# A block's opening on one Trainium2 core: tokens transposed before their shift, three heads of the first block first, queues in written order

## The chip, the cores and the metric

The kernel runs on one core of a Trainium2 chip: TensorE (PE) multiplies into PSUM, VectorE (DVE), ScalarE (ACT) and GpSimd (POOL) do the elementwise work, and SyncE (SP) issues the DMAs. One launch computes the whole result from inputs in HBM. The metric is the device time of the launch in microseconds; the time before is 3143.29 us, the median of three runs (3138.22 to 3143.47).

## The reference

A transformer block with adaptive layer norm on x of 2048 tokens by 576 channels, all fp32:

```python
mod = (_silu(c) @ w_mod).reshape(c.shape[0], 6, 1, -1)
sa, ca, ga, sb, cb, gb = ...            # six rows of 576
h = _layernorm(x) * (1 + ca) + sa
x = x + ga * attention(h)               # 32 heads of 128 over 16 K/V groups, the last 512 cached keys
h = _layernorm(x) * (1 + cb) + sb
x = x + gb * ((sigmoid(h @ w_gate) * (h @ w_up)) @ w_down)      # 4608 wide
```

In the attention each head's queries are `h @ wq`, the scores are scaled by `Dh ** -0.5`, a softmax follows over the 512 keys, and the heads' outputs go through `wo`.

## The kernel before, in words

Tokens are in four blocks of 512, each of four tiles of 128; the 576 channels are four chunks of 128 and a tail of 64. Products of fp32 precision are made from three products of rounded halves: an operand is split into a rounded part ("hi", a ScalarE copy) and the rest ("lo", a subtraction on DVE or POOL).

**Opening (lines 79 to 289).** 16 products on zeros warm TensorE up (L90). `silu(c)` is spread over 128 columns (`sbc`, L104), so that a row of w_mod comes out on all partitions: ten fp32 products a row (L282), for scale (m = 1) and then shift (m = 0); DVE copies them out (L285). For block 0, `ln_stats` and `ln_rsqrt` make mean and reciprocal root on DVE, `ln_apply` normalizes, multiplies by scale and adds shift (L176 to L178), and `ln_transpose` turns the tile over on TensorE (L191, L192) and splits it into `hTm` and `hTt` (L194 to L197). The gate row (m = 2) is made otherwise: ScalarE multiplies w_mod by silu(c), POOL sums the chunks, and a product with ones spreads it (`mod_sum`, `mod_half`).

**Attention (lines 292 to 718).** `seq` lists 128 pairs of head and block, the instances b. A step n is one tile i of an instance: b, i = divmod(n, 4). The loop at L702 runs the steps; in step n it calls a quarter of the projection of instance b + 2 (`qproj`; from step -7 on for the first), the scores of tile n + 2, the transposes of the softmax's tile n, a quarter of P times V of the instance before, and two products with Wo of the one before that. `scores` also has DVE's maximum (`neg`, L362) and ScalarE's exponential (`pp`, L364); `transp` has ScalarE's copy and DVE's subtraction (`ptt`, L378, L379). Scores, transposes of P and of K share three PSUM banks (`st`); Wo's products have two (`wo`).

What is done ahead (loads, splits of weights, K and V preparation, the normalization of later blocks) is entered with `at_n(step, function, ...)` in `at_step` and called at the start of its step, before that step's products. Each load takes one of four raw buffers (`raw_tile`, L73), which come free when their last reader is done, in the order of the steps.

```python
at_n(max(q_first(hh) - 16, NLO), load_q, hh)
at_n(max(q_first(hh) - 8, NLO + 1), split_q, hh)
at_n(n - 7, make_k, gg)
norm_block(1, -12, -3, -2, 1, scale, shift, nc.vector, nc.vector)
```

The order on an engine is set by the framework's scheduler, except for instructions given to `tc.keep_in_program_order` (`pin`): these keep the written order among themselves on their engine. Each engine runs its queue strictly in order, and so does SP.

**Background.** While the attention runs, 135 jobs combine and split the weights of the second stage and store them to DRAM (`bg_load` to `bg_store`, L592 to L678), one job every three steps (`slots`, L681), from step 4 in the first half and from step 300 in the second. Every ninth of the first 81 is a "tail" job, which loads four small column blocks in twelve DMAs.

The second stage (from L724) is the gated unit; nothing in it is changed.

## Time and profile before

| what | value |
|---|---|
| median of three runs | 3143.29 us (3138.22 to 3143.47) |
| profiled execution | 3142.64 us, its span 3140.8 us |
| PE busy | 3070.3 us (98%) |
| DVE, ACT, POOL busy | 2165.6, 1455.5, 1561.7 us |
| DMA | 501.73 MB, mean 160 GB/s |

The span is the time from the first instruction to the last of the profiled execution; the 1.8 us around it belong to the launch. TensorE's busy time counts its products with modelled ends, so its share says where it waits, not how near it is to its peak. The first fortieth of the span (78.5 us) is the only one with a busy share of TensorE under eight tenths.

### The profile page before, as it was taken

Reading aid. Unit: us, or ns where it says so; the run is one execution under the profiler, and the core shown is the slowest. Engines: PE = TensorE matmul, PEld = TensorE weight load, DVE = VectorE, ACT = ScalarE, POOL = GpSimd, SP = SyncE. Lnnn points to the kernel's source line nnn. Section 1 sums busy time; section 2 is a strip of 40 time slices with the busy share of each in tenths; the row PEclk is TensorE's granted clock in tenths of the full one; section 3 lists DMA queues with packets and bytes.
Section 4 is the critical chain, followed back from the end, with each engine's and each line's share of the span. In section 5 each row is a group of like instructions: output and inputs, shape, how many; then the busy total and the mean of one; then the engine's idle time right before and its main releaser. Section 6 shows DMA issues by size and latency. Waiting matters only on the chain.

```text
span 3140.8 us, 50879 instructions
## 1 busy us (share of the span) xinstructions
PE 3070.3 (98%) x17012; PEld 2653.1 (84%) x17012; DVE 2165.6 (69%) x4202; ACT 1455.5 (46%) x3189; POOL 1561.7 (50%) x1937
## 2 busy tenths in 40 slices
...
GB/s 143 152 171 149 150 158 173 144 157 154 119 31 94 65 87 154 136 117 125 110 118 111 110 121 253 251 249 214 198 197 202 219 245 200 198 201 198 198 202 119
DMA packets 576740, 501.73 MB, mean 160 GB/s; under 512 B 193504, under 2 KB 456672, under 8 KB 575456
## 3 DMA queue, kind: packets, MB, share of 16 engines
...
q8 instruction: 135, 2.21, 0.3%
...
## 4 chain that ended last, share of the span: by engine, by line
PE 84%; POOL 4%; issue 4%; DVE 3%; DMA 3%; SPq 2%; ACT 1%; POOLq 0%; DVEq 0%; ACTq 0%
PE a L878 14%; PE w L249 12%; PE qp L249 11%; PE wo L249 11%; PE ot L249 10%; PE st L249 9%; PE c L878 7%; PE st L375 6%; PE b L878 3%; SPq L668 1%; DMA raw<-in_A_v_cache_dram 1%; POOL x L657 1%; DVE x L850 0%; POOL hl L809 0%; POOL wb L241 0%
## 5 line engine op out<-in xcount | busy, mean ns | idle before, releaser
L850 DVE TENSOR_TENSOR x<-w,x 128x288 f32<-128x288 f32 x980 | 443.7, 456 | 462.6 <-PE w L249 462.0
L249 PE MATMUL wo<-wb,ov 128*128 128x288 f32 x3072 | 619.7, 310 | 3.7 <-DVE x L402 1.6
L378 ACT ACTIVATE ptt<-st 128x512 fp32r<-128x512 f32 x512 | 305.8, 597 | 619.1 <-PE st L375 618.9
L249 PEld LDWEIGHTS w<-sd,hl 128*128 128x128 f32 x3036 | 514.0, 189 | 89.4 <-POOL hl L809 5.1
L878 PE MATMUL a<-hc,sw 128*128 128x512 f32 x2016 | 583.7, 394 | 2.4 <-DVE v L1015 1.7
L249 PE MATMUL w<-sd,hl 128*128 128x288 f32 x3036 | 563.7, 295 | 3.6 <-POOL hl L809 3.2
L402 DVE SCALAR_TENSOR_TENSOR x<-wo,rs,x 128x288 f32<-128x288 f32 x1024 | 513.3, 512 | 61.6 <-PE wo L249 12.1
L362 DVE TENSOR_REDUCE neg<-st 128x1 f32<-128x512 f32 x512 | 352.6, 689 | 284.2 <-PE st L249 281.7
L249 PEld LDWEIGHTS wo<-wb,ov 128*128 128x128 f32 x3072 | 485.1, 190 | 53.4 <-DVE x L402 3.1
L249 PE MATMUL qp<-hTm,wa 128*128 128x512 f32 x1536 | 446.1, 399 | 6.5 <-DVE qt L346 4.0
L249 PE MATMUL ot<-ptt,vs 128*128 128x512 f32 x1536 | 445.5, 398 | 0.1
L249 PE MATMUL st<-kt,qt 128*128 128x512 f32 x1536 | 438.7, 394 | 0.9 <-DVE hTm L195 0.6
L878 PEld LDWEIGHTS a<-hc,sw 128*128 128x128 f32 x2016 | 355.7, 188 | 42.1 <-DVE v L1015 3.3
L379 DVE TENSOR_TENSOR ptt<-st,ptt 128x512 fp32r<-128x512 f32 x512 | 348.4, 681 | 36.2 <-ACT ptt L378 36.1
L364 ACT ACTIVATE pp<-st,neg 128x512 f32<-128x512 f32 x512 | 349.9, 683 | 33.2 <-DVE neg L362 29.6
L249 PEld LDWEIGHTS st<-kt,qt 128*128 128x128 f32 x1536 | 288.5, 188 | 64.1 <-DVE ptt L379 1.0
L375 PEld LDWEIGHTS st<-ident,pp 128*128 128x128 f32 x2048 | 254.9, 140 | 90.2 <-ACT pp L364 23.3
L375 PE MATMUL st<-ident,pp 128*128 128x128 f32 x2048 | 308.9, 273 | 17.3 <-ACT pp L364 17.0
L878 PE MATMUL c<-hc,sw 128*128 128x512 f32 x1008 | 305.9, 396 | 11.5 <-ACT v L885 11.5
L241 POOL TENSOR_TENSOR wb<-raw,wb 128x576 fp32r<-128x576 f32 x64 | 91.3, 1427 | 448.6 <-ACT wb L237 445.6
L249 PEld LDWEIGHTS qp<-hTm,wa 128*128 128x128 f32 x1536 | 262.8, 190 | 34.1 <-DVE qt L346 5.4
L249 PEld LDWEIGHTS ot<-ptt,vs 128*128 128x128 f32 x1536 | 261.4, 189 | 23.7 <-DVE ptt L379 0.3
...
## 6 DMA issues: line engine op xcount, KB each, us to landing
...
sd<-dsc SPq DMA_DIRECT2D x249, 288.0 KB, 2.9
...
dsc<-x SPq DMA_DIRECT2D x126, 96.0 KB, 2.4
```

The costliest lines, as they stand in the source:

```text
L241: pin(nc.gpsimd.tensor_sub(sp[:, 1, :], raw, f32(sp[:, 0, :])))
L249: nc.tensor.matmul(p, l, r, start=first and n == 0, stop=last and n == len(pairs) - 1)
L362: nc.vector.tensor_reduce(NEG[b][:, i : i + 1], p, axis=AX.X, op=OP.max, negate=True)
L364: nc.scalar.activation(PP[n], p, AF.Exp, bias=NEG[b][:, i : i + 1], accum_out=SUM[b][:, i : i + 1])
L375: nc.tensor.transpose(p[:, k * P : (k + 1) * P], PP[n][:, k * P : (k + 1) * P], ident)
L378: nc.scalar.activation(PT[b][:, 0, :, cols], pv_, AF.Copy)
L379: nc.vector.tensor_sub(PT[b][:, 1, :, cols], pv_, f32(PT[b][:, 0, :, cols]))
L402: nc.vector.scalar_tensor_tensor(xv, p, RS[b][:, i : i + 1], xv, op0=OP.mult, op1=OP.add)
L657: pin(nc.gpsimd.tensor_sub(v.bitcast(F32R), v, hi[:, a:b, :]))
L668: pin(nc.sync.dma_start(wsc[f + q][to * TQ : (to + 1) * TQ, a:b, 4, :], src[rows]))
L850: nc.vector.tensor_add(acc, p, acc)
L878: nc.tensor.matmul(p, l, r, start=first and n == 0, stop=n == len(pairs) - 1, skip_group_check=not first)
```

## The change

- `Ordered` wraps the handle of the engines: while `held[0]` is true, every instruction issued through it is kept in written order. It turns false at step 8; from there only what was pinned before is kept.
- Block 0's tokens are normalized on ScalarE (`ln_scaled`: x times y plus a bias of -mean times y), multiplied by scale, and transposed without the shift. The channels then lie on partitions, and the shift, turned over into columns (`scol`), is added as a per-partition bias when the transposes are copied from PSUM (`ln_shifted`), for a whole chunk of 512 tokens at once. Block 1 goes the same way in steps -1 to 6.
- All w_mod rows, gate too, are made by ten fp32 products; the gate's are spread over the opening and steps -3, 2 and 3. The loads are issued in another order, x in four pieces behind two chunks of w_mod.
- `seq` begins with heads 0, 1 and 2 on block 0, then head 2 on block 1, heads 0 and 1 on block 1, head 3 on both. K's second group is so needed from instance 2 on, prepared at step 4, and heads 0 and 1 need their Wo twice (`inst`: 66 Wo instances where there were 64).
- Steps run from -8 instead of -24, head 3's projection is in steps 7 and 8, the background's first slot is step 7, and 10 warm-up products are left of 16.

```diff
+class Ordered:
...
+    def __init__(self, tc, held, of, deep=True):
+        self._tc, self._held, self._of, self._deep = tc, held, of, deep
+    def __getattr__(self, name):
+        got = getattr(self._of, name)
+        if self._deep:
+            return Ordered(self._tc, self._held, got, False)
+        def call(*args, **kw):
+            i = got(*args, **kw)
+            if self._held[0]:
+                self._tc.keep_in_program_order(i)
+            return i
+        return call
...
-    nc = tc.nc
+    held = [True]
+    nc = Ordered(tc, held, tc.nc)
...
+    def pin(i):
+        if not held[0]:
+            tc.keep_in_program_order(i)
...
-    for k in range(16):
+    for k in range(10):
         nc.tensor.matmul(idle[:, :P], busy, busy, start=True, stop=True)
...
-    load_x(0)
+    sbc = at.tile([P, NC + 1, P], F32, tag="ov", name="sbc", bufs=2)
+    nc.vector.tensor_copy(sbc, cexp[:, :, None].to_broadcast([P, NC + 1, P]))
+    extra = at.tile([P, 4 * P], F32, tag="extra", name="extra")
     scale, shift, gate = mod_rows("scale", wp), mod_rows("shift", wp), mod_rows("gate", wp)
-    wm = {}
-    for m in (1, 0):
-        w = at.tile([P, NC + 1, D], F32, tag="ptt", name="wm0", bufs=2)
-        for k in range(NC + 1):
+    WM, EARLY, HN, NMR = {}, {}, {}, {}
+    def load_mod(m, ks):
+        if m not in WM:
+            WM[m] = at.tile([P, NC + 1, D], F32, tag="ptt", name="wm0", bufs=2)
+        for k in ks:
             kk = P if k < NC else TAIL
-            nc.sync.dma_start(w[:kk, k, :], w_mod[k * P : k * P + kk, m * D : (m + 1) * D])
-        wm[m] = w
+            nc.sync.dma_start(WM[m][:kk, k, :], w_mod[k * P : k * P + kk, m * D : (m + 1) * D])
+    def mod_mm(m, ks, p2):
+        for k in ks:
+            kk = P if k < NC else TAIL
+            for j in range(2):
+                nc.tensor.matmul(p2[j], sbc[:kk, k, :], WM[m][:kk, k, j * D2 : (j + 1) * D2],
+                                 start=(k == 0), stop=(k == NC))
+    def ln_ready(b):
+        ln_rsqrt(b)
+        mv, y = LN[b]
+        NMR[b] = const.tile([P, TPB], F32, tag="ln_a", name="nmr", bufs=2)
+        nc.vector.scalar_tensor_tensor(NMR[b], mv[:, :, 0], -1.0, y, op0=OP.mult, op1=OP.mult)
+    def ln_scaled(b, t, eng):
+        h = wp.tile([P, D], F32, tag="h", name="h", bufs=4)
+        nc.scalar.activation(h, xs[b][:, t, :], AF.Identity, scale=LN[b][1][:, t : t + 1],
+                             bias=NMR[b][:, t : t + 1])
+        eng.tensor_mul(h, h, scale)
+        HN[b, t] = h
+    def ln_tail(b, t):
+        e = extra[:, t * P : (t + 1) * P].rearrange("p (s d) -> p s d", s=2)
+        nc.gpsimd.tensor_copy(e, HN[b, t][:, None, NC * P :].to_broadcast([P, 2, TAIL]))
+    def ln_channels(b, t, k, p):
+        src = HN[b, t][:, k * P : (k + 1) * P] if k < NC else extra[:, t * P : (t + 1) * P]
+        nc.tensor.transpose(p[:, t * P : (t + 1) * P], src, ident)
+    def ln_shifted(b, k, p):
+        main, tail = hTs[b]
+        hi, lo = (main[:, k, :], main[:, NC + k, :]) if k < NC else (tail[:, 0, :], tail[:, 1, :])
+        nc.scalar.activation(hi, p, AF.Identity, bias=scol[:, k : k + 1])
+        nc.vector.scalar_tensor_tensor(lo, p, scol[:, k : k + 1], f32(hi), op0=OP.add, op1=OP.subtract)
...
+    load_mod(1, range(2))
+    for t in range(TPB):
+        nc.sync.dma_start(xs[0][:, t, :], xf[0][:, t, :])
+    load_mod(1, range(2, NC + 1))
+    load_mod(0, range(NC + 1))
+    EARLY["q", 0] = load_a(wq, 0)
+    p2 = [ps_wo(), ps_wo()]
+    mod_mm(1, range(NC + 1), p2)
+    load_mod(2, range(2))
+    EARLY["q", 1] = load_a(wq, DH)
+    EARLY["k"] = load_k0()
+    load_x(1)
+    EARLY["q", 2] = load_a(wq, 2 * DH)
+    load_mod(2, range(2, NC + 1))
     for t in range(TPB):
         ln_stats(0, t)
-    ln_rsqrt(0)
-    for m, row, add in ((1, scale, 1.0), (0, shift, 0.0)):
-        p2 = [ps_wo(), ps_wo()]
+    for j in range(2):
+        nc.scalar.activation(scale[:, j * D2 : (j + 1) * D2], p2[j], AF.Copy, bias=1.0)
+    ln_ready(0)
+    for t in range(TPB):
+        ln_scaled(0, t, nc.vector)
+        ln_tail(0, t)
+    cols = [ps_pt(), ps_pt(), ps_pt(), ps_ot(), ps_ot()]
+    p2 = [ps_wo(), ps_wo()]
+    mod_mm(0, range(NC), p2)
+    for t in range(TPB):
         for k in range(NC + 1):
-            kk = P if k < NC else TAIL
+            ln_channels(0, t, k, cols[k])
+        if t == 0:
+            mod_mm(0, (NC,), p2)
+    nc.scalar.activation(shift[:, :D2], p2[0], AF.Copy)
+    nc.vector.tensor_copy(shift[:, D2:], p2[1])
+    ends = wp.tile([P, 2, TAIL], F32, tag="hd", name="hd", bufs=1)
+    nc.scalar.activation(ends, p2[1][:, None, D2 - TAIL :].to_broadcast([P, 2, TAIL]), AF.Copy)
+    pc = ps_qp()
+    for k in range(NC + 1):
+        src = shift[0:1, k * P : (k + 1) * P] if k < NC else ends.rearrange("p s d -> p (s d)")[0:1, :]
+        nc.tensor.transpose(pc[:, k : k + 1], src, ident[0:1, 0:1])
+    scol = csb
+    nc.vector.tensor_copy(scol, pc[:, : NC + 1])
+    EARLY["sq"] = split_a_hi(EARLY["q", 0])
+    split_a_lo(EARLY["q", 0], EARLY["sq"])
+    new_hT(0)
+    for k in range(NC + 1):
+        ln_shifted(0, k, cols[k])
+    gate2 = [ps_wo(), ps_wo()]
+    mod_mm(2, range(1), gate2)
+    def gate_mm(ks):
+        mod_mm(2, ks, gate2)
+        if NC in ks:
             for j in range(2):
-                nc.tensor.matmul(p2[j], sbc[:kk, k, :], wm[m][:kk, k, j * D2 : (j + 1) * D2],
-                                 start=(k == 0), stop=(k == NC))
-        for j in range(2):
-            nc.vector.tensor_scalar(row[:, j * D2 : (j + 1) * D2], p2[j], add, None, op0=OP.add)
-    new_hT(0)
-    for t in range(TPB):
-        ln_apply(0, t, scale, shift, nc.vector, nc.vector)
-        ln_transpose(0, t)
+                nc.scalar.activation(gate[:, j * D2 : (j + 1) * D2], gate2[j], AF.Copy)
+    def chunks1(ks):
+        if 0 in ks:
+            new_hT(1)
+        for k in ks:
+            p = ps_wide()
+            for t in range(TPB):
+                ln_channels(1, t, k, p)
+            ln_shifted(1, k, p)
...
-            if hd in (0, H - 2):
+            if half == 0 and hd < 4:
+                if hd == 0:
+                    seq += [(0, 0, 0), (0, 1, 0), (0, 2, 0), (0, 2, 1), (0, 0, 1), (0, 1, 1), (0, 3, 0), (0, 3, 1)]
+            elif hd in (0, H - 2):
                 seq += [(half, hd, b0), (half, hd + 1, b0), (half, hd, b1), (half, hd + 1, b1)]
             else:
                 seq += [(half, hd, b0), (half, hd, b1), (half, hd + 1, b0), (half, hd + 1, b1)]
...
-    NLO = -24
+    NLO = -8
...
+    SA[0], RA[1], RA[2], KR[0] = EARLY["sq"], EARLY["q", 1], EARLY["q", 2], EARLY["k"]
+    at_n(-8, load_v, 0)
+    at_n(-4, split_q, 1)
+    at_n(-4, split_q_lo, 1)
+    at_n(-3, make_k, 0)
+    at_n(-3, gate_mm, (1,))
+    at_n(-1, split_q, 2)
+    at_n(-1, split_q_lo, 2)
+    at_n(3, split_q, 3)
+    at_n(3, split_q_lo, 3)
+    for t in range(TPB):
+        at_n(-1 + t // 2, ln_stats, 1, t)
+    at_n(1, ln_ready, 1)
+    for t in range(TPB):
+        at_n(2 + t // 2, ln_scaled, 1, t, nc.vector if t % 2 else nc.gpsimd)
+    at_n(2, gate_mm, (2,))
+    at_n(3, gate_mm, (3, 4))
+    for t in range(TPB):
+        at_n(4, ln_tail, 1, t)
+    at_n(5, chunks1, (0, 1))
+    at_n(6, chunks1, (2, 3, 4))
...
-    for hh in range(1, NH):
-        at_n(max(q_first(hh) - 16, NLO), load_q, hh)
-        at_n(max(q_first(hh) - 8, NLO + 1), split_q, hh)
-        at_n(max(q_first(hh) - 7, NLO + 1), split_q_lo, hh)
+    def o_first(i):
+        return TPB * (inst[i][1] + 2)
+    def o_free(i):
+        return TPB * (inst[i][2] + 3)
+    for hh in range(3, NH):
+        at_n(max(q_first(hh) - 16, -6), load_q, hh)
+        if hh > 3:
+            at_n(q_first(hh) - 8, split_q, hh)
+            at_n(q_first(hh) - 7, split_q_lo, hh)
     for gg in range(2 * HKV):
         n = TPB * first_g[gg]
         if gg:
             at_n(n - 15, load_k, gg)
-            at_n(n - 7, make_k, gg)
+            at_n(n - 7 if gg > 1 else 4, make_k, gg)
             at_n(n - 10, load_v, gg)
-        at_n(n - 2, make_v, gg)
...
-    at_n(-6, mod_fetch, 2)
-    at_n(-3, lambda: mod_sum(wm[2]))
-    for j in range(2):
-        at_n(j, mod_make, gate, 2, j, 0.0)
-    for hh in range(NH):
-        n = max(o_first(hh) - 7, o_free(hh - 2) if hh > 1 else 0)
+        at_n(n - 2 if gg else 1, make_v, gg)
+    for hh in range(len(inst)):
+        n = max(o_first(hh) - 7, o_free(hh - 2) if hh > 1 else 5)
         assert n < o_first(hh)
         at_n(n - 7, load_o, hh)
-        at_n(max(n - 3, 1), scale_o, hh)
+        at_n(max(n - 3, 4), scale_o, hh)
         at_n(n, split_o, hh)
         at_n(n, split_o_lo, hh)
...
-    norm_block(1, -12, -3, -2, 1, scale, shift, nc.vector, nc.vector)
...
-    slots = [(n, 0) for n in range(4, n1 - 43, STEP)] + [(n, 1) for n in range(n1 + 44, N - 14, STEP)]
+    slots = [(n, 0) for n in range(7, n1 - 43, STEP)] + [(n, 1) for n in range(n1 + 44, N - 14, STEP)]
...
+        if n == 2 * TPB:
+            held[0] = False
         for fn, args in at_step.pop(n, ()):
             fn(*args)
         b, i = divmod(n, TPB)
         bq, part = divmod(n - 1, TPB)
-        if ok(bq + 2):
+        if bq + 2 == 3:
+            if n > 6:
+                qproj(3, 2 * (n - 7))
+                qproj(3, 2 * (n - 7) + 1)
+        elif ok(bq + 2):
             qproj(bq + 2, part)
```

How this moves the instructions is shown at three places. Names carry a number where one tile is told from another; L36 is the wrapper's line.

ScalarE in the changed kernel, steps 1 to 4 (`h`: block 1's normalization, `pp`: exponentials, `ptt`: P's hi copy, `wa`: the split of Wq's head 3, `gate`: the gate row):

```order
L36 ACTIVATE h<-x_102,nmr,ln_y 128x576 [waits DMAHW1_49,Pool_49]
L36 ACTIVATE h<-x_102,nmr,ln_y 128x576 [waits Pool_49]
L36 ACTIVATE pp,sum<-st,neg 128x512 [waits DVE_49,PE_49,Activation_49]
L36 ACTIVATE ptt<-st 128x4x128
L36 ACTIVATE wa<-raw 128x640 [waits DMAHW7_49,DMAHW6_49,DMAHW5_49]
L36 ACTIVATE h<-x_102,nmr,ln_y 128x576 [waits Pool_49] x2
L36 ACTIVATE gate<-wo 128x288 [waits PE_49] x2
L36 ACTIVATE pp,sum<-st,neg 128x512 [waits DVE_49,PE_49,Activation_49]
L36 ACTIVATE ptt<-st 128x4x128
L36 ACTIVATE kt<-st 128x512 [waits PE_49]
L36 ACTIVATE qt<-qp 128x512 [waits PE_49]
```

ScalarE before, around its third Wq split (`wa`), among block 1's copies and the modulation's multiplications (`wmt`):

```order
L378 ACTIVATE ptt<-st 128x4x128 [waits PE_49]
L212 ACTIVATE wa<-raw 128x640 [waits DMAHW7_49,DMAHW0_49,Pool_49]
L126 ACTIVATE wmt<-wmt,cexp 64x288 [waits DMAHW3_49,Activation_49]
L185 ACTIVATE hd<-h 128x128 [waits DVE_49]
L126 ACTIVATE wmt<-wmt,cexp 64x288
L364 ACTIVATE pp,sum<-st,neg 128x512 [waits DVE_49]
L194 ACTIVATE hTm<-st 128x4x128 [waits PE_49]
L196 ACTIVATE hTt<-wo 128x128 [waits PE_49]
L237 ACTIVATE wb<-raw 128x576 [waits Pool_49]
L364 ACTIVATE pp,sum<-st,neg 128x512 [waits DVE_49,PE_49]
L378 ACTIVATE ptt<-st 128x4x128
L378 ACTIVATE ptt<-st 128x4x128 [waits PE_49]
```

The split of a Wq head, which stood among other copies, now stands in written order ahead of two normalizations, the gate's copies and the exponential of tile 5.

SP in the changed kernel, from V's first load: `raw_345` is K's second group, `raw_472` is Wq's head 3, which takes the buffer that `raw_345` leaves (its DMA queue 1, and PE's transposes):

```order
L36 DMA raw_343<-in_A_v_cache_dram 128x512 [waits DMAHW0_49,Activation_49,Pool_49]
L36 DMA raw_345<-in_A_k_cache_dram 128x512 [waits DMAHW1_49,Activation_49,Pool_49]
L36 DMA raw_383<-in_A_v_cache_dram 128x512 [waits DMAHW2_49,PE_49]
L36 DMA raw_385<-in_A_wo_dram 128x576 [waits DMAHW3_49,DMAHW4_49,Activation_49,Pool_49]
L36 DMA raw_387<-in_A_wo_dram 128x576 [waits DMAHW0_49,Pool_49]
L36 DMA raw_472<-in_A_wq_dram 128x4x128 [waits DMAHW5_49,DMAHW1_49,PE_49]
L36 DMA raw_472<-in_A_wq_dram 64x128 [waits DMAHW6_49]
L36 DMA raw_472<-in_A_wq_dram 64x128 [waits DMAHW7_49]
```

SP before, from V's first load: `raw_344` and `raw_384` are Wq's second and third head:

```order
L317 DMA raw_342<-in_A_v_cache_dram 128x512 [waits DMAHW2_49,DVE_49,PE_49]
L202 DMA raw_344<-in_A_wq_dram 128x4x128 [waits DMAHW3_49,DVE_49,PE_49]
L204 DMA raw_344<-in_A_wq_dram 64x128 [waits DMAHW4_49]
L204 DMA raw_344<-in_A_wq_dram 64x128 [waits DMAHW5_49]
L118 DMA wmt_396<-in_w_mod_dram 64x576 [waits DMAHW6_49,PE_49,Activation_49]
L202 DMA raw_384<-in_A_wq_dram 128x4x128 [waits DMAHW7_49,DMAHW2_49,Pool_49]
L204 DMA raw_384<-in_A_wq_dram 64x128 [waits DMAHW0_49]
L204 DMA raw_384<-in_A_wq_dram 64x128 [waits DMAHW1_49]
L232 DMA raw_398<-in_A_wo_dram 128x576 [waits PE_49]
```

The load that waited for POOL's split of V in before is, for head 3, now one that waits for TensorE's transposes of K.

DVE in the changed kernel, from the first scores' maximum (`neg`) on: block 1's statistics (`BN_STATS`, `BN_AGGR`) stand between the maxima:

```order
L36 TENSOR_REDUCE neg<-st 128x1 [waits PE_49]
L36 BN_STATS st<-x_102 128x6 [waits DMAHW1_49]
L36 BN_STATS st<-x_102 128x6
L36 BN_AGGR mv<-st 128x2 [waits DVE_49]
L36 BN_STATS st<-x_102 128x6 x2
L36 BN_AGGR mv<-st 128x2 [waits DVE_49]
L36 TENSOR_REDUCE neg<-st 128x1 [waits PE_49]
L36 BN_STATS st<-x_102 128x6 x2
L36 BN_AGGR mv<-st 128x2 [waits DVE_49]
L36 BN_STATS st<-x_102 128x6 x2
L36 BN_AGGR mv<-st 128x2 [waits DVE_49]
L36 SCALAR_TENSOR_TENSOR qt<-qp,qt 128x512 [waits Activation_49]
```

DVE before, from the last copies of block 0 on: the same statistics ahead of any scores:

```order
L195 TENSOR_TENSOR hTm<-st,hTm 128x4x128 [waits Activation_49]
L197 TENSOR_TENSOR hTt<-wo,hTt 128x128 [waits Activation_49]
L326 TENSOR_TENSOR kt<-st,kt 128x512 [waits Activation_49]
L158 BN_AGGR mv<-st 128x2 [waits DVE_49]
L155 BN_STATS st<-x_110 128x6 x2
L155 BN_STATS st<-x_110 128x6 [waits DVE_49]
L158 BN_AGGR mv<-st 128x2 [waits DVE_49]
L155 BN_STATS st<-x_110 128x6
L158 BN_AGGR mv<-st 128x2 [waits DVE_49]
L164 TENSOR_SCALAR ln_v<-mv 128x4 [waits DVE_49]
```

The statistics of block 1 moved from ahead of the first scores to between the first three, and the reciprocal root behind them.

## Rows read from the trace of the kernel before

**Rows 1.** Busy time by stretch; columns: engine busy (instructions), granted clock, DMA share, GB/s.

```profile
0.00:58.50 58.50, 41.52 (x169) 30.39 (x169) 46.26 (x110) 24.18 (x59) 15.92 (x21) 0.85 0.51 158
58.50:200.00 141.50, 141.50 (x798) 121.58 (x799) 105.00 (x193) 88.37 (x206) 77.41 (x110) 1.00 0.50 134
```

**Rows 2.** TensorE's timeline, opening; columns: start us, us, engine line op, idle before.

```profile
8.55 5.28 PE L282 MATMUL wo<-wm,raw 128*128 128x288 f32 x20 [1.28 <-DMA wm<-in_w_mod_dram]
...
29.41 0.80 PE L249 MATMUL qp<-hTm,wa 128*128 128x512 f32 x1 [1.31 <-ACT wa L212]
30.77 5.06 PE L249 MATMUL qp<-hTm,wa 128*128 128x512 f32 x11 [0.56 <-POOL wa L216]
...
44.89 1.63 PE L249 MATMUL st<-kt,qt 128*128 128x512 f32 x3
```

**Rows 3.** TensorE's timeline, after the opening.

```profile
74.83 0.84 PE L249 MATMUL st<-kt,qt 128*128 128x512 f32 x3
...
77.45 0.60 PE L323 MATMUL st<-ident,raw 128*128 128x128 f32 x4
```

**Rows 4.** Chain of waits: start us, us, what.

```profile
70.43 0.44 PE st L375 x4
70.87 0.70 PE ot L249 x3
```

**Rows 5.** Groups of instructions, 0 to 80 us: count | busy us, mean ns | idle before.

```profile
L362 DVE TENSOR_REDUCE neg<-st 128x1 f32<-128x512 f32 x12 | 8.2, 687 | 4.6 <-PE st L249 4.5
L364 ACT ACTIVATE pp<-st,neg 128x512 f32<-128x512 f32 x11 | 7.5, 683 | 0.7 <-DVE neg L362 0.7
...
L379 DVE TENSOR_TENSOR ptt<-st,ptt 128x512 fp32r<-128x512 f32 x9 | 6.2, 688 | 2.4 <-ACT ptt L378 2.4
...
L378 ACT ACTIVATE ptt<-st 128x512 fp32r<-128x512 f32 x10 | 6.0, 598 | 8.5 <-PE st L375 8.5
...
L212 ACT ACTIVATE wa<-raw 128x640 fp32r<-128x640 f32 x4 | 2.8, 729 | 0.0
```

**Rows 6.** DVE's timeline: statistics, reciprocal root, multiplications of blocks 0 and 1.

```profile
7.55 1.18 DVE L155 BATCH_NORM_STATS2 st<-x 128x6 f32<-128x288 f32 x3 [2.17 <-DMA x<-in_A_x_dram]
...
13.20 0.16 DVE L171 SCALAR_TENSOR_TENSOR ln_y<-ln_a,ln_y 128x4 f32<-128x4 f32 x1
...
15.12 1.41 DVE L177 TENSOR_TENSOR h<-h,scale 128x576 f32<-128x576 f32 x2
...
39.89 2.63 DVE L177 TENSOR_TENSOR h<-h,scale 128x576 f32<-128x576 f32 x2
```

**Rows 7.** POOL's timeline beside the last of these.

```profile
37.87 2.77 POOL L129 TENSOR_TENSOR wm<-wm 128x288 f32<-128x288 f32 x3 [4.70 <-ACT wm L126]
```

**Rows 8.** Two-microsecond stretches of the opening; columns as in rows 1.

```profile
20.00:22.00 2.00, 0.85 (x8) 0.81 (x9) 1.97 (x4) 0.50 (x2) 0.00 (x0) 1.00 0.77 252
22.00:24.00 2.00, 1.76 (x10) 0.87 (x8) 1.90 (x5) 2.00 (x7) 0.00 (x0) 0.76 0.43 102
...
28.00:30.00 2.00, 0.69 (x2) 0.29 (x1) 1.82 (x6) 1.86 (x4) 0.56 (x1) 0.50 0.71 180
...
42.00:44.00 2.00, 0.06 (x1) 0.09 (x2) 2.00 (x3) 0.12 (x1) 1.92 (x2) 0.88 0.00 0
44.00:46.00 2.00, 2.00 (x8) 1.81 (x9) 2.00 (x2) 1.62 (x5) 1.84 (x3) 0.50 0.00 0
...
50.00:52.00 2.00, 0.43 (x4) 0.42 (x4) 2.00 (x5) 2.00 (x6) 0.00 (x0) 1.00 0.00 0
```

**Rows 9.** SP's timeline: the two small pieces of a Wq load.

```profile
33.62 1.15 SPq L204 DMA_DIRECT2D raw<-in_A_wq_dram  x2
```

**Rows 10.** Raw buffers, 0 to 60 us: landing times of their loads.

```profile
DMA to landing us min/median/max: 2.3/4.1/7.3
```

**Rows 11.** A stall in the middle of the attention.

```profile
530.00:540.00 10.00, 6.17 (x28) 5.16 (x27) 3.79 (x7) 4.27 (x11) 7.43 (x11) 0.75 0.52 144
```

**Rows 12.** ScalarE's waits from 450 to 800 us: us, times, longest.

```profile
ACT x L652 <- POOL extra L639: 5.0, 1, 5.0
```

50 lines of the change are left out of this document (25 added, 25 removed).

## The prediction

> **What bounds the kernel now.** I read the busy times by stretch first. In the first 58.5 us TensorE is busy 41.5 us at a mean clock of 0.85; in the next 141.5 us it is busy all of them at 1.00 [rows 1]. So from 58.5 us on the end is set by TensorE's own work, and the change, which rearranges the opening, is worth what it shifts the moment from which TensorE never waits, no more. The reader is to see in TensorE's timeline how late that moment comes: first projection at 29.4 us, first scores at 44.9 [rows 2]; the eleventh scores (tile 10) start at 74.8, in the stretch without a gap [rows 3]. I use "tile 10 starts" as the milestone: by then both kernels have done the same attention work, except that the one before still owes the transposes of its second K group (four, at 77.5), 0.44 us at the pitch of the chain of waits, where three products of a 512-column group take 0.70, 0.23 each [rows 3, 4]. So before stands at 75.3 us, and whatever the changed kernel reaches there later or earlier is the change in the end time, all work after it being the same.
>
> **The opening up to the first scores: about 15 us earlier.** A w_mod row is ten products of 0.53 us [rows 2]. With two of its chunks ahead of x in SP's queue and three behind, the first row ends at about 12.5 us (estimate); ScalarE's two copies free its banks at 13.6. Four chunks of the second row take 4.2 us, to 17.8; the transposes of token tile 0, now from the unshifted h, 0.55; the last chunk 1.06; the other three tiles 1.65: 21.1. Five column transposes and a DVE copy end at 21.9, one ScalarE copy and one DVE subtraction (0.60 and 0.69, like the copies of P [rows 5]) open the first projection at 23.4. Before, it started at 29.4 [rows 2]. Fourteen products go at DVE's pace, to 26.7; K's transposes 0.44, one gate chunk 1.06 and seven products 1.6 bring tile 0's scores to 29.9, against 44.9. The six warm-up products left out fall in time that waits for loads anyway: nothing.
>
> **The steps after it: given back.** What was done early (statistics, normalization and transposes of block 1) now lies between the scores, in written order on every queue. With that order each step is one loop through DVE and ScalarE: DVE's maximum of tile n+2 (0.69), ScalarE's exponential (0.69), ScalarE's copy of the transposed tile n (0.60), DVE's subtraction (0.69): 2.7 us with hand-over [rows 5], and what stands between them is added. At full clock TensorE has 1.8 to 3.9 us of work in such a step, so up to step 7 the loop decides, not TensorE.
> - Step 0: scores 0 end at 30.6. Before scores 2's maximum DVE has two more reductions, the statistics of four token tiles and the split of q: the whole of statistics and reciprocal root took 5.8 us for block 0 (7.55 to 13.36) [rows 6], some 3.4 of it the statistics, which I take at 4.0 among the others: maximum done at 37.2, copy of tile 0 done at 38.5.
> - Step 1: loop 2.7 and the root with its thirteen small operations, 2.5: 43.7.
> - Step 2: two ScalarE normalizations 1.2, a DVE multiplication and 2.0 of the loop. The multiplication is 0.71 where POOL is idle and 1.31 where POOL adds [rows 6, 7]; POOL works on its own two tiles here, so I take 1.31: 48.2.
> - Step 3 holds a new wait. ScalarE's next instruction is the split of Wq's head 3. Its load takes the raw buffer of K's second group, so SP can issue it only behind that group's transposes, which stand in step 4, behind DVE's subtraction of tile 2. ScalarE cannot pass it: behind the split stand two normalizations, two gate copies and exponential 5, and TensorE's scores 6 need the bank that exponential 5 frees. Transposes end at 49.4; three DMAs take 1.5 to issue (the last two 1.15 [rows 9]) and 2.3 to 4.1 to land [rows 10]. I take 2.3, since the last ones are the 32 KB pieces: 53.3 (bounds 53.0 and 55.1). ScalarE so stands still for 5 us and TensorE for some 8. Then split 0.73 [rows 5], normalizations 1.2, multiplication 1.3, loop 2.0: 58.5.
> - Step 4: loop and two more subtractions on DVE, K's and q's, each some 0.6 (0.69 less what the next one overlaps): 3.8, 62.3. Step 5: two for block 1's first chunks, 3.8: 66.1. Step 6: three, 4.5: 70.6. Step 7: the bare loop, 2.7: 73.3.
> - Then TensorE's remaining projection of 1.6 us; tile 10 starts at about 75.2.
>
> Against 75.3 that is 0. The 15 us of lead are spent: about 6.5 on statistics and root inside the loop, 5 on the wait for head 3, the rest on block 1's chunks.
>
> **Other parts.** Gate as ten fp32 products instead of two costs some 4 us more of TensorE, all inside steps where the loop is late: nothing; if that cover went, 4. Two more Wo instances (heads 0 and 1 are used twice) add two loads, two POOL multiplications and two splits beside other work, on engines with slack: nothing, 0 to 1. The background work on the second stage's weights begins one slot (three steps) later and takes one slot more in the second half. Its four-column "tail" jobs move by three steps against K's pattern of sixteen. Before, the fifth of them (step 28 + 4 x 27 = 136) sat one step ahead of a K preparation (9 x 16 - 7 = 137), and will be at 139; TensorE lost 3.8 us in those 10 us, at clock 0.75 [rows 11], while ScalarE waited 5.0 us for POOL's sums [rows 12]. That one goes; another may take its place. I bound it by -4 and +4 and take 0.
>
> **Clock.** Before, the granted clock was 0.50 (the 1.2 GHz level) at 28 to 30 us, after TensorE had worked 0.85 of 2 us at 20 to 22, and again at 44 to 46, after 0.06 of 2 at 42 to 44; yet it stayed 1.00 at 50 to 52 with 0.43 of 2 [rows 8]. In the changed order TensorE is busy nearly all the time from 13.6 to 34, so I expect 2.4 GHz for the first projections, and the low level after the wait of 8 us. From scores 6 to 64 us that costs 1.1, to 72 us 3.5; to 60 nothing, the loop being later. I take 1.
> The Trainium skill (TensorE: Matmul & The Clock Gate, "HAM oscillation — how this bites in real kernels") says that waits between bursts throttle the clock, so that each burst begins slow. The first two stretches agree with it, the third doesn't; by the rule the sum is the +1 to +3.5 above, by the third stretch 0.
>
> **Sum.** 0 + 1 = 1 us on the profiled execution's 3142.6 (span 3140.8 and 1.8 around it), which is 0.65 below the median shown; I say 3143.5.
>
> **Rivals.**
> - Faster: the wait for head 3 is short or hidden. Without its 5 us, and without the low clock behind it, tile 10 starts at 69.7, so 5.6 earlier: 3137; with the tail job's 4 us gone as well, 3133. For it: the lead at the first scores is real in every count. Against: the new instruction order shows load, transposes and split in just this dependence, and exponential 5 behind it.
> - Slower: the clock falls to 1.2 GHz at the first projection and comes back only after it, as in the kernel before (0.76 at 22 to 24 us, 0.50 at 28 to 30 [rows 8]). Place: 24 to 36 us; price: 21 products at 0.46 (5.06 us for 11 [rows 2]) instead of 0.23, four transposes and a gate chunk at double, 6 us, all on the path, since the first scores head the loop: 3149.5; with Wq landing at 4.1 us instead of 2.3, 3151. Each us at the low level costs half a us there, so it decides from some 12 us on. For it: TensorE waits around 22 us for the shift's columns. Against: some 1 us of waiting there, where before it had worked 0.85 of 2 us [rows 8].
> - The loop is longer than counted: POOL beside DVE stretches more than the two multiplications. Each 0.6 us on the loop is 0.6 us of time; five such are 3 us: 3146.
>
> **Numbers.** Given back, within some 4 us of 3143.5: 0.66 (its own range 3139 to 3148, with the longer loop in it). Faster: 0.15, of which 0.13 beyond 6.3 us. Slower: 0.19, of which 0.17 beyond. 0.2% of 3143 us, 6.3 us, is about what a measurement of this kernel tells from no change. So faster 0.13, same 0.70, slower 0.17; range 3135 to 3152, which reaches into both rivals and holds the tail job's bounds.
>
> **What would show it.** Right: first scores near 30 us; ScalarE idle for about 5 us before Wq's third-head split, released by a DMA; TensorE idle for 7 to 8 us near 50 to 58 us; the never-waiting stretch beginning past 66 us; tile 10 near 75. Wrong: no such idle time (then faster), or a clock of 0.50 between 24 and 36 us (then slower). The step most open is the landing of Wq and what the clock does behind it; time lost or won behind 80 us, near 530 us first [rows 11], would be the background's part.

## The result: slower by a quarter of a percent, and the profile after

The changed kernel's median is 3150.15 us (3144.04 to 3152.09, seven runs), the kernel before beside it 3138.22 us (3135.7 to 3146.7, seven runs): ratio 1.0025, 95% interval 1.0015 to 1.0034, some 7.8 us. The profiled execution took 3150.36 us, its span 3148.3 against 3140.8. That is inside the range forecast, but it is a loss, and the forecast was none. By the 6.3 us that the prediction itself drew between no change and slower, it lies on the slower side, to which it had given 0.17.

TensorE's timeline of the changed kernel answers to [rows 2, 3]. All instructions that are held in written order show line 36, the wrapper's.

```profile
11.08 7.70 PE L36 MATMUL wo<-wm,sbc 128*128 128x288 f32 x28 [2.75 <-DMA wm<-in_w_mod_dram]
...
24.54 2.99 PE L36 MATMUL qp<-hTm,wa 128*128 128x512 f32 x12 [0.69 <-DVE hTm L36]
...
31.12 0.84 PE L36 MATMUL st<-kt,qt 128*128 128x512 f32 x3
...
51.30 0.66 PE L36 MATMUL st<-ident,raw 128*128 128x128 f32 x4 [0.56 <-DVE ptt L36]
...
60.22 1.65 PE L36 MATMUL st<-kt,qt 128*128 128x512 f32 x3 [7.33 <-ACT pp L36]
...
70.53 0.63 PE L36 MATMUL wo<-ident,extra 128*128 128x128 f32 x4 [2.44 <-DVE hTm L36]
...
73.80 2.40 PE L36 MATMUL qp<-hTm,wa 128*128 128x512 f32 x7
...
79.51 0.86 PE L36 MATMUL st<-kt,qt 128*128 128x512 f32 x3
```

The first scores come at 31.1 us, 13.8 us ahead of before; tile 10's at 79.5, 4.2 us behind the 75.3 of before (with its owed transposes). The lead is spent, and more. From there on both kernels have scores every 3.4 us; at tile 16, where nothing is owed any more, they stand at 100.0 and 95.8, still 4.2 apart. The other 3.3 of the 7.5 us between the spans come later. Tile 16's scores, in the changed kernel and before:

```profile
100.00 0.85 PE L36 MATMUL st<-kt,qt 128*128 128x512 f32 x3
```

```profile
95.84 0.84 PE L249 MATMUL st<-kt,qt 128*128 128x512 f32 x3
```

ScalarE's timeline shows where it went (`pp` the exponential, `ptt` the copy of the transposed tile, `wa` the split of Wq):

```profile
38.30 0.69 ACT L36 ACTIVATE pp<-st,neg 128x512 f32<-128x512 f32 x1 [1.86 <-DVE neg L36]
38.89 0.19 ACT L36 ACTIVATION_READ_ACCUMULATOR pp<-st,neg 128x1 f32 x1
38.98 0.59 ACT L36 ACTIVATE ptt<-st 128x512 fp32r<-128x512 f32 x1
...
44.42 0.69 ACT L36 ACTIVATE pp<-st,neg 128x512 f32<-128x512 f32 x1 [4.33 <-DVE neg L36]
...
49.93 0.59 ACT L36 ACTIVATE ptt<-st 128x512 fp32r<-128x512 f32 x1
55.45 0.74 ACT L36 ACTIVATE wa<-raw 128x640 fp32r<-128x640 f32 x1 [4.93 <-DMA raw<-in_A_wq_dram]
...
59.39 0.69 ACT L36 ACTIVATE pp<-st,neg 128x512 f32<-128x512 f32 x1 [1.10 <-DVE neg L36]
```

Two things stand in it. The split of head 3 waits 4.93 us for its load, and TensorE 7.33 us behind it. And the copy of tile 0, whose transposes ended at 35.4, starts at 38.98: it stands behind the exponential of tile 2, which waits for DVE's maximum. The groups of 0 to 80 us sum that up, against 0.7 us of such waiting of the exponentials and 2.4 of DVE's subtractions before [rows 5]:

```profile
L36 ACT ACTIVATE pp<-st,neg 128x512 f32<-128x512 f32 x10 | 6.9, 688 | 20.2 <-DVE neg L36 19.7 <-PE wo L36 0.4
...
L36 DVE TENSOR_TENSOR ptt<-st,ptt 128x512 fp32r<-128x512 f32 x8 | 5.5, 692 | 9.1 <-ACT ptt L36 9.1
```

By stretch, as in [rows 1, 8, 11]:

```profile
0.00:58.50 58.50, 43.58 (x189) 32.49 (x189) 30.53 (x83) 22.92 (x43) 13.27 (x21) 0.97 0.52 159
58.50:200.00 141.50, 137.34 (x765) 118.53 (x766) 102.99 (x189) 89.81 (x206) 84.37 (x114) 0.97 0.46 126
...
38.00:40.00 2.00, 2.00 (x6) 1.52 (x6) 0.58 (x2) 1.70 (x4) 0.00 (x0) 0.50 0.08 29
...
58.00:60.00 2.00, 0.00 (x0) 0.00 (x0) 1.27 (x2) 0.90 (x3) 1.92 (x3) 0.52 0.43 121
60.00:62.00 2.00, 1.78 (x5) 1.34 (x6) 1.31 (x3) 1.63 (x5) 2.00 (x5) 0.50 0.58 157
...
72.00:74.00 2.00, 2.00 (x8) 1.71 (x7) 1.27 (x2) 1.02 (x3) 1.52 (x2) 0.50 0.83 253
```

```profile
530.00:540.00 10.00, 7.63 (x43) 6.27 (x41) 4.21 (x8) 2.85 (x8) 8.57 (x11) 1.00 0.59 165
540.00:550.00 10.00, 8.51 (x40) 7.22 (x41) 6.78 (x12) 6.13 (x16) 6.48 (x10) 0.83 0.44 122
```

Up to 58.5 us TensorE does more than before and at a better clock; behind it 4.2 us are idle where before had none. The granted clock stands at its lower level (0.50) at 38 to 40, 60 to 64 and 72 to 74 us, behind waits of 2.30, 7.33 and 2.44 us; behind the wait of 2.75 us before 11.08 it stayed at 1.00. Near 530 us TensorE still loses 3.9 us, as it did before (3.83): that stall has only moved.

### The profile page after: what moved, and what is told of

Its sections match the earlier page's. It is cut to its first block, busy times and chain, and to the rows that moved or that the text cites. A ratio compares the mean times of both kernels' runs of the same rounds, so it can differ in the third digit from the quotient of the medians.

```text
span 3148.3 us, 50886 instructions
## 1 busy us (share of the span) xinstructions
PE 3069.1 (97%) x17021; PEld 2653.4 (84%) x17021; DVE 2149.1 (68%) x4176; ACT 1459.5 (46%) x3181; POOL 1566.2 (50%) x1943
## 4 chain that ended last, share of the span: by engine, by line
PE 84%; DVE 4%; POOL 4%; DMA 3%; SPq 2%; issue 2%; ACT 1%; POOLq 0%; ACTq 0%; DVEq 0%
PE st L36 16%; PE a L36 13%; PE w L36 12%; PE wo L36 12%; PE qp L36 11%; PE ot L36 10%; PE c L36 7%; PE b L36 3%; SPq L36 2%; DVE x L36 1%; POOL x L36 1%; DMA ts<-scr 1%; POOL h L36 1%; POOL extra L36 0%; POOL hl L36 0%
## 5 line engine op out<-in xcount | busy, mean ns | idle before, releaser
L36 DVE TENSOR_TENSOR x<-w,x 128x288 f32<-128x288 f32 x980 | 444.6, 457 | 466.3 <-PE w L36 465.1
L36 PE MATMUL wo<-wb,ov 128*128 128x288 f32 x3072 | 619.6, 310 | 4.4 <-DVE ov L36 2.2
L36 PEld LDWEIGHTS w<-sd,hl 128*128 128x128 f32 x3036 | 513.1, 189 | 89.8 <-POOL hl L36 5.4
L36 PE MATMUL a<-hc,sw 128*128 128x512 f32 x2016 | 582.9, 393 | 3.6 <-DVE v L36 2.1
L36 ACT ACTIVATE ptt<-st 128x512 fp32r<-128x512 f32 x512 | 306.2, 598 | 601.4 <-PE st L36 600.7
L36 PE MATMUL w<-sd,hl 128*128 128x288 f32 x3036 | 565.2, 296 | 3.8 <-POOL hl L36 3.5
L36 DVE SCALAR_TENSOR_TENSOR x<-wo,rs,x 128x288 f32<-128x288 f32 x1024 | 513.4, 512 | 58.4 <-PE wo L36 9.4
L36 DVE TENSOR_REDUCE neg<-st 128x1 f32<-128x512 f32 x512 | 352.7, 689 | 278.2 <-PE st L36 276.1
L36 PEld LDWEIGHTS wo<-wb,ov 128*128 128x128 f32 x3072 | 483.8, 189 | 53.7 <-DVE ov L36 3.2
L36 PE MATMUL qp<-hTm,wa 128*128 128x512 f32 x1536 | 446.2, 399 | 5.8 <-DVE qt L36 5.2
L36 PE MATMUL st<-kt,qt 128*128 128x512 f32 x1536 | 438.1, 393 | 7.6 <-ACT pp L36 7.3
L36 PE MATMUL ot<-ptt,vs 128*128 128x512 f32 x1536 | 445.3, 397 | 0.1
L36 PEld LDWEIGHTS a<-hc,sw 128*128 128x128 f32 x2016 | 355.3, 188 | 43.4 <-DVE v L36 3.7
L36 DVE TENSOR_TENSOR ptt<-st,ptt 128x512 fp32r<-128x512 f32 x512 | 348.9, 681 | 44.9 <-ACT ptt L36 44.8
L36 ACT ACTIVATE pp<-st,neg 128x512 f32<-128x512 f32 x512 | 350.2, 684 | 55.1 <-DVE neg L36 52.9
L36 PEld LDWEIGHTS st<-kt,qt 128*128 128x128 f32 x1536 | 289.5, 189 | 72.6 <-ACT pp L36 7.8
L36 PEld LDWEIGHTS st<-ident,pp 128*128 128x128 f32 x2048 | 254.7, 140 | 91.9 <-ACT pp L36 26.1
L36 PE MATMUL st<-ident,pp 128*128 128x128 f32 x2048 | 308.2, 273 | 21.1 <-ACT pp L36 21.0
L36 POOL TENSOR_TENSOR wb<-raw,wb 128x576 fp32r<-128x576 f32 x66 | 94.1, 1427 | 469.5 <-ACT wb L36 469.4
L36 PE MATMUL c<-hc,sw 128*128 128x512 f32 x1008 | 305.3, 396 | 12.0 <-ACT v L36 12.0
L36 POOL TENSOR_TENSOR x<-x,x 128x128 fp32r<-128x128 f32 (+7 forms) x458 | 270.7, 605 | 60.4 <-ACT x L36 39.6
L36 PEld LDWEIGHTS qp<-hTm,wa 128*128 128x128 f32 x1536 | 263.0, 190 | 32.8 <-DVE qt L36 6.5
```

The lines of the kernel that those rows point to most:

```text
L36: i = got(*args, **kw)
```

## The experiments

Times of single executions scatter by several us here, so the table gives the ratio of the runs to those of the kernel before on the same chip, and three distances from each profile: from the first projection (P) to the scores of tiles 8, 10 and 16, which leave out how late P itself is. The ratios' intervals are some 0.0009 to either side, so a difference between two of them is uncertain by some 0.0013, 4 us (an estimate from the intervals shown).

| kernel | ratio, 95% | P, us | P to tile 8 | P to tile 10 | P to tile 16 |
|---|---|---|---|---|---|
| before | 1 | 29.4 | – | 45.9 with the 0.44 owed | 66.4 |
| changed | 1.0025 (1.0015 to 1.0034) | 24.5 | 46.4 | 55.0 | 75.5 |
| late_split | 1.0007 (0.9998 to 1.0016) | 27.6 | 41.7 | 50.8 | 71.4 |
| k1_early | 1.0012 (1.0003 to 1.0021) | 26.3 | 41.0 | 47.9 | 69.0 |
| stats_early | 1.0020 (1.0011 to 1.0029) | 24.3 | 46.2 | 53.2 | 74.2 |
| unheld | 0.9969 (0.9958 to 0.9981) | 27.5 | 28.6 | 36.7 | 59.1 |
| copy_first | 1.0013 (1.0004 to 1.0023) | 23.8 | 42.0 | 50.6 | 71.1 |
| copy_first_late | 0.9998 (0.9987 to 1.0009) | 29.3 | 37.5 | 44.4 | 64.9 |
| slot4 | 1.0021 (1.0012 to 1.0030) | 25.0 | 46.3 | 54.9 | 75.9 |
| unheld_warm16 | 0.9981 (0.9971 to 0.9991) | 25.1 | 28.6 | 36.7 | 61.1 |
| spread | 0.9989 (0.9980 to 0.9998) | 24.0 | 33.9 | 42.5 | 63.0 |
| spread_stats | 0.9979 (0.9970 to 0.9988) | 27.4 | 33.8 | 42.4 | 62.9 |
| unheld_b | 0.9987 (0.9978 to 0.9996) | 26.5 | 28.6 | 36.7 | 62.2 |
| unheld_warm16_b | 0.9980 (0.9971 to 0.9989) | 29.0 | 28.6 | 36.6 | 61.0 |

Before has no figure at tile 8, since its projection of head 3 lies earlier. From tile 8 to tile 10 lie 7.0 us in the profiles whose granted clock stays at 1.00 there (k1_early, stats_early, copy_first_late), and 8.5 to 9.1 where it falls to 0.50 (the changed kernel, late_split, copy_first, slot4). So some 1.6 us of a distance to tile 10 are the clock's, and differ between profiles whatever the edit; the distance to tile 8 is the better one to compare. The scores of tiles 8 and 10 in the changed kernel, then in k1_early:

```profile
70.92 0.95 PE L36 MATMUL st<-kt,qt 128*128 128x512 f32 x3
...
79.51 0.86 PE L36 MATMUL st<-kt,qt 128*128 128x512 f32 x3
```

```profile
67.22 0.94 PE L36 MATMUL st<-kt,qt 128*128 128x512 f32 x3
...
74.19 0.85 PE L36 MATMUL st<-kt,qt 128*128 128x512 f32 x3
```

### late_split: head 3's split two steps later

```diff
-    at_n(3, split_q, 3)
-    at_n(3, split_q_lo, 3)
+    at_n(5, split_q, 3)
+    at_n(5, split_q_lo, 3)
```

> One part undone: the split of Wq's head 3 is called at step 5 instead of step 3, so it stands behind exponentials 5 and 6 in ScalarE's queue; its load and the buffer it takes stay as they are. Theory A (the wait for that load costs the time): ScalarE's idle time of 4.9 us before the split goes, TensorE's idle time before scores 6 falls from 7.3 us to under 3, the low clock at 58 to 66 us goes with it, tile 10's scores start at 71 to 74 us instead of 79.5, and the time falls by 6 to 8 us, to that of the kernel before (ratio to it 0.9995 to 1.0010). Theory B (the written order makes each step's loop through DVE and ScalarE too long, whatever waits in it): the 5 us that are not waited for are waited for elsewhere, as the loop of the steps 3 to 7 gives them back; tile 10 at 78 or later, ratio 1.002 to 1.003. Theory C (the background work, moved by one slot, costs the time): tile 10 earlier, but the time unchanged, ratio 1.002 or more.

TensorE's scores 6, which waited 7.33 us:

```profile
58.03 0.97 PE L36 MATMUL st<-kt,qt 128*128 128x512 f32 x3 [2.06 <-ACT pp L36]
```

The wait is 2.06 us and the products are at full clock (0.97 for three instead of 1.65). P to tile 8 falls by 4.7 us, to tile 10 by 4.2 (the low clock comes here at 68 to 74 us), and the ratio by 0.0018, 5.7 us: as theory A has it, a little under its price. Tile 10 itself, at 78.3, misses the 71 to 74 expected, for 3.0 us of which the opening is answerable (P at 27.6, below). So the wait is a cause; with it gone the kernel is still not faster than before.

### k1_early: the same wait taken away through the buffer

```diff
-            at_n(n - 7 if gg > 1 else 4, make_k, gg)
+            at_n(n - 7 if gg > 1 else 0, make_k, gg)
```

> The same wait taken away by another way: K's second group is transposed in step 0 instead of step 4, so that the raw buffer it holds is free some 10 us earlier and Wq's head 3 is loaded before ScalarE comes to its split, which stays at step 3. The price is that DVE's and ScalarE's work on K (a copy and a subtraction of 512 columns) and four transposes lie in step 0's loop. Theory A: no idle time of ScalarE for a DMA before the split, scores 6 some 4 to 6 us earlier than 60.2, tile 10 at 73 to 77 us, time 3 to 6 us under the changed kernel's. Theory B: step 0's loop gets longer by 1.3 us or more, and the loop of the other steps decides as before: tile 10 at 78 or later. Theory C: time unchanged.

The Wq load is issued at 43.87 us instead of 51.99, and ScalarE's split no longer waits:

```profile
52.74 0.74 ACT L36 ACTIVATE wa<-raw 128x640 fp32r<-128x640 f32 x1
```

7.1 us less from P to tile 10, 5.4 to tile 8, 0.0013 in the ratio (4.1 us): the size A gave; scores 6, at 53.8, come 6.4 us earlier, a little more than its 4 to 6. Two different edits that share only the removed wait gain alike, 4 to 6 us by the ratios and 4.7 and 5.4 us at tile 8. So the wait is a cause, of about that size, though the ratio of k1_early alone is only just apart from the changed kernel's; and the load's earlier issue shows that the buffer held by K's second group made it.

### stats_early: block 1's statistics ahead of the first scores

```diff
-        at_n(-1 + t // 2, ln_stats, 1, t)
-    at_n(1, ln_ready, 1)
+        at_n(-3, ln_stats, 1, t)
+    at_n(-3, ln_ready, 1)
```

> One part moved: block 1's statistics and reciprocal root are called at step -3, ahead of the first scores, instead of steps -1 to 1, where DVE does them between the maxima of tiles 1 to 4. Theory B (what stands in the loop costs the time): scores 0 a little later or equal (31.1 to 33), then steps 0 and 1 shorter by about 6 us together, tile 10 at 74 to 77 us, time 3 to 5 us under the changed kernel's. Theory A (the wait for head 3 is the price, and its end hangs on K's second group, which hangs on the loop): the whole moves only by what the steps ahead of K's transposes gain, net of the later first scores, some 2 us: tile 10 at 77 to 78, ScalarE still idle for 4 to 6 us before the split, time 1 to 3 us less.

First scores at 30.9, tile 10 at 77.5, and TensorE waits 7.18 us for ScalarE's exponential as in the changed kernel. 1.8 us less from P to tile 10, ratio 1.0020: the 2 us of theory A, not the 6 of B. But up to tile 8 the two kernels differ by only 0.2 us, and the rest is step 7, where this profile has the full clock. Nor was the work taken off the chain. DVE still does the statistics and the root ahead of the first maximum, which starts at 35.95 us where it started at 32.00:

```profile
35.95 1.28 DVE L36 TENSOR_REDUCE neg<-st 128x1 f32<-128x512 f32 x2
```

So this run says that the place of the statistics in DVE's queue hardly matters here; what they cost it does not say.

### unheld: the same work, order left to the scheduler

```diff
-    held = [True]
+    held = [False]
```

> The written order alone undone: the same work in the new places, but only the instructions that were kept in order in the kernel before are kept, the scheduler orders the rest. Theory B (the written order itself costs the time): the steps 0 to 2 shorten, K's second group is transposed at 48 us or earlier instead of 51.3, tile 10 at 76 us or earlier, time 3 to 8 us under the changed kernel's. Theory A (the wait for head 3 costs it, and it is one of buffers): ScalarE or TensorE still stands for 4 us or more on the load of head 3 or on what replaces it, time within 3 us of the changed kernel's. The scheduler can also order the opening worse than it is written: first scores later than 33 us would show that.

P to tile 10 falls to 36.7 us, and the kernel is faster than before. Here is how ScalarE runs, beside the timeline above:

```profile
42.17 0.60 ACT L36 ACTIVATE ptt<-st 128x512 fp32r<-128x512 f32 x1 [0.18 <-PE st L36]
42.67 0.69 ACT L36 ACTIVATE pp<-st,neg 128x512 f32<-128x512 f32 x1
```

```profile
L36 ACT ACTIVATE pp<-st,neg 128x512 f32<-128x512 f32 x14 | 9.6, 687 | 4.7 <-DVE neg L36 4.7
```

The copy of tile n now stands ahead of exponential n + 2, and the exponentials wait 4.7 us in all instead of 20.2. This goes beyond what B expected (18 us in the profile and by the ratios, 12 by the ratio of `unheld_b`, against 3 to 8), and it mixes causes: in this order head 3's load also finds another buffer, issued at 44.17, ahead of K's transposes at 48.67. The next runs take it apart.

### copy_first and copy_first_late: one pair of instructions turned round

```diff
         if 0 <= n + 2 < N:
-            scores(n + 2)
+            p = scores(n + 2)
         if 0 <= n < N:
             transp(n)
+        if n < 2 * TPB and n + 2 >= 0:
+            exps(n + 2, p)
```

(`exps` is the end of `scores`, the exponential and the reciprocal of the sums; `copy_first_late` also has the later split.)

> One order undone on ScalarE: in steps -2 to 7 exponential n + 2 is issued behind transp(n), so that the copy of the transposed tile n stands ahead of it in ScalarE's queue, as the scheduler puts it when nothing is held (with it DVE's reciprocal of the sums moves behind one subtraction); all else is held in written order, and head 3's load stays as late as it is. From the first projection to tile 10's scores the changed kernel takes 55.0 us, the one without held order 36.7. Theory D (the written order costs the time because the copy of tile n waits behind the maximum and the exponential of tile n + 2): the copies of tiles 0 to 2 come 1 to 4 us earlier each, K's second group is transposed at 45 to 48 us instead of 51.3, the load of head 3 lands that much earlier, and the 55.0 us fall to 42 to 48; time 7 to 12 us under the changed kernel's (ratio to before 0.9985 to 1.0005). Theory A (the load of head 3 alone): its 5 us of waiting stay whole, since the buffer comes free through the same chain; 51 us or more, time at most 4 us less. Theory E (it is the buffers that the scheduler gives out otherwise, not the order of copies): no change, 54 to 56 us.

> Both at once, all else held in written order: the copy of tile n ahead of exponential n + 2, and the split of head 3 at step 5. Theory D with A (the two together are what the held order costs): 36 to 41 us from the first projection to tile 10's scores, time within 4 us of the one without held order (ratio to before 0.996 to 0.9985). Theory E, or a third part in the order of DVE's small operations: 45 us or more, time not under before's.

ScalarE of `copy_first`:

```profile
35.57 0.59 ACT L36 ACTIVATE ptt<-st 128x512 fp32r<-128x512 f32 x1
...
51.47 0.74 ACT L36 ACTIVATE wa<-raw 128x640 fp32r<-128x640 f32 x1 [4.22 <-DMA raw<-in_A_wq_dram]
```

The copy of tile 0 comes 3.4 us earlier (2.6 counted from P), K's second group is transposed at 47.5, and P to tile 10 is 50.6: less gain (4.4 us) than D's 42 to 48, more than E's none, and just past A's bound of 51. The wait of 4.22 us for head 3 is still there. With both undone it is 44.4 us, 10.5 less than the changed kernel where the two alone gave 4.4 and 4.2. That looks as if each hid part of the other's gain, but it is the clock between tiles 8 and 10: at tile 8 the two alone give 4.4 and 4.7 us and both together 8.9, and by the ratios 3.8, 5.7 and 8.5 us. The gains add up. The ratio 0.9998 is that of before, not the 0.996 to 0.9985 of D with A: a third part was missing.

### slot4: the background one slot earlier again

```diff
-    slots = [(n, 0) for n in range(7, n1 - 43, STEP)] + ...
+    slots = [(n, 0) for n in range(4, n1 - 43, STEP)] + ...
```

> The background's first slot back at step 4 from 7, all else as in the changed kernel: the tail jobs stand again at step 136 and its like. Theory C (the move of the slots costs time): behind 80 us TensorE's idle time falls below the changed kernel's 55.2 us by 2 us or more, and the time by as much. What I expect: the stalls near 530 and 1040 us move within 10 us and stay 3 to 5 us each, idle time 52 to 57 us, time within 2 us of the changed kernel's (ratio to before 1.002 to 1.003); the two added jobs in the opening's steps could cost up to 1.

```profile
530.00:540.00 10.00, 8.07 (x45) 6.59 (x43) 4.43 (x9) 2.84 (x7) 8.58 (x11) 1.00 0.65 182
540.00:550.00 10.00, 8.09 (x38) 7.03 (x39) 6.67 (x12) 6.60 (x16) 6.46 (x10) 0.83 0.44 121
```

TensorE loses the same 3.8 us there, and the ratio is 1.0021. TensorE's idle time from 80 to 3140 us is 48.9 us against 55.2, 6 us less by theory C's measure, but the ratio falls by 0.0004 only, 1 us. So C is not supported as a cause of the loss; with 4 us of uncertainty, a part of some us isn't excluded either.

### spread and spread_stats: the third part

```diff
-    at_n(5, chunks1, (0, 1))
-    at_n(6, chunks1, (2, 3, 4))
+    at_end = {4: (0, 1), 5: (2, 3), 6: (4,)}
...
             wo_acc(b - 2, i, 1)
+        if n in at_end:
+            chunks1(at_end[n])
```

(both on top of `copy_first_late`; `spread_stats` also has, over `spread`)

```diff
-        at_n(-1 + t // 2, ln_stats, 1, t)
-    at_n(1, ln_ready, 1)
+        at_n(-4 + t // 2 * 2, ln_stats, 1, t)
+    at_n(0, ln_ready, 1)
```

> On top of the copy ahead of the exponential and the later split: block 1's chunks are called behind P times V at the end of the steps 4 (chunks 0 and 1), 5 (2 and 3) and 6 (tail), near the places where the scheduler puts them, instead of ahead of the scores of the steps 5 and 6; all still held in written order. From the first projection to tile 10's scores the version with two parts undone takes 44.4 us, the one without held order 36.7. Theory G (the chunks, as a block ahead of the scores, are the third part): scores 8 come at most 33 us behind the first projection instead of 37.5, tile 10 at 39 to 41 us behind it, time 2 to 5 us less than with the two parts (ratio to before 0.998 to 0.9995). Theory H (the statistics and the reciprocal root on DVE in steps -1 to 1 are the third part): 43 to 45 us, no change in time.

> The same, and block 1's statistics in DVE's idle time ahead of the first scores (two tiles at step -4, two at -2) with the reciprocal root at step 0, as the scheduler puts them. Theories G and H both in part: 36 to 39 us from the first projection to tile 10's scores, so that the written order, mended at four places, does as well as the one without it; time within 3 us of that (ratio to before 0.996 to 0.998). If G alone holds, no gain over the run with the chunks moved; if 41 us or more are left, there is a fifth part that I have not named.

With the chunks behind the scores, scores 8 come 33.9 us behind P instead of 37.5 and tile 10 42.5 instead of 44.4: G's direction at about half its size, with a ratio of 0.9989, whose interval overlaps that of copy_first_late. The statistics moved again leave the distance as it is (42.4), so H adds nothing that the profile shows; the ratios of the two overlap. The root still stands there ahead of the third maximum (36.92 to 40.63 us). By its own expectation, 41 us or more leave a further part that isn't named. Written order mended at three places so runs as fast as the order left to the scheduler on the same chip (0.9989 and 0.9979 beside 0.9987 and 0.9980), though tile 10 still comes 5.8 us later behind P. Why that does not show in the time, the next runs tell.

### unheld_warm16, unheld_b and unheld_warm16_b: the opening's clock, and what the scheduler's order loses

(The edit stands on top of that of `unheld`; `unheld_b` is `unheld` and `unheld_warm16_b` is `unheld_warm16` once more.)

```diff
-    for k in range(10):
+    for k in range(16):
         nc.tensor.matmul(idle[:, :P], busy, busy, start=True, stop=True)
```

> The version without held order and with 16 warm-up products instead of 10, as the kernel before had. In the three runs whose TensorE waited 3.1 to 3.8 us for the third chunk of w_mod, the granted clock fell and the 28 products took 9.2 to 10.9 us; in the two that waited 2.3 to 2.8 us they took 7.7 to 7.9. Six more products last some 2.7 us and leave a wait of under 1 us. Theory F (that wait costs up to 3 us by the clock): the 28 products take 7.5 to 8 us, first projection at 24 to 25 us instead of 27.5, time 2 to 3 us under the version with 10. Rival: the products that come later start later by what the clock would have lost, or the landing of w_mod is what sets the products' pace: no change within 1 us.

> The version without held order once more, beside the ones mended in written order and the one with 16 warm-up products on the same chip: before, it ran on another chip and six times only. If its 3131.5 us were the chip's or chance, it comes to 3134 to 3137 here, as the one with 16 did; if they are its own, to 3130 to 3133 (ratio to before 0.996 to 0.998).

> The version with 16 warm-up products once more, on the same chip as the one with 10. By the first projection alone (25.1 us against 27.5 in the two profiles) it should be 2 to 3 us faster; in the first comparison, on another chip, it was 4 us slower, 5 us of it behind tile 10, where the two have the same instructions but for names and some order. Theory F (the clock in the opening) predicts 1 to 3 us faster than with 10 on the same chip; the rival, that the difference behind tile 10 belongs to the kernel, predicts 3 to 5 us slower; no difference within 1.5 us would say that the opening's gain is lost again behind it.

Left to the scheduler, the kernel does reach tile 10 first, and waits right behind it. ScalarE and TensorE of `unheld_b`:

```profile
68.74 0.53 ACT L36 ACTIVATE wmt<-wmt,cexp 64x288 f32<-64x288 f32 x1 [4.68 <-DMA wmt<-in_w_mod_dram]
69.18 0.57 ACT L36 ACTIVATE ptt<-st 128x512 fp32r<-128x512 f32 x1
```

```profile
70.54 0.99 PE L36 MATMUL st<-ident,pp 128*128 128x128 f32 x4 [3.14 <-DVE ptt L36]
```

A piece of w_mod for the second stage stands ahead of a copy in ScalarE's queue, and its load has not landed: 4.68 us of ScalarE, 3.14 of TensorE. So at tile 16 `unheld_b` is only 0.8 us ahead of `spread`. The second comparison brings 0.9987 where the first had 0.9969: part of the first lead was chance or the chip's, as that run's expectation had it for 3134 to 3137 (3136.97).

The 16 warm-up products did not settle the clock. In the first profile the third chunk was waited for 1.40 us and the clock stayed full; in the second:

```profile
8.00:10.00 2.00, 0.65 (x3) 0.19 (x1) 1.77 (x6) 0.00 (x0) 0.00 (x0) 1.00 1.04 386
10.00:12.00 2.00, 1.33 (x4) 0.68 (x5) 1.79 (x9) 0.00 (x0) 0.00 (x0) 0.90 1.05 242
12.00:14.00 2.00, 2.00 (x4) 1.17 (x4) 1.37 (x9) 0.32 (x1) 0.00 (x0) 0.50 1.05 370
```

it fell behind a wait of 1.94 us, and the 28 matmul instructions (two to a product) took 12.65 us. In `slot4`, whose TensorE did less in the same stretches, it stayed:

```profile
8.00:10.00 2.00, 0.26 (x2) 0.00 (x0) 1.74 (x6) 0.00 (x0) 0.00 (x0) 1.00 1.02 388
10.00:12.00 2.00, 0.40 (x2) 0.35 (x3) 1.86 (x8) 0.00 (x0) 0.00 (x0) 1.00 1.08 277
12.00:14.00 2.00, 2.00 (x9) 1.20 (x8) 1.66 (x11) 0.00 (x0) 0.00 (x0) 1.00 1.03 336
```

Theory F fails as a rule. On one chip the version with 16 is 1.6 us ahead by its median; that lies within F's 1 to 3, but it is less than the intervals can tell apart, and P came later in its profile (29.0 against 26.5), not earlier. Both times it is faster than before, by 0.0019 and 0.0020; it and `spread_stats` are some 6 us under before and 14 under the changed kernel.

## Why the prediction was right in its mechanism and off in its sum

- **What bounds.** Right as far as tile 16: from tile 10 on the changed kernel keeps a pace of 3.3 to 3.5 us per tile, and the 4.2 us read at tile 10 are still 4.2 at tile 16. Behind it a further 3.3 us come (below).
- **Opening.** Forecast first scores at 29.9, came at 31.1. The step that was short is the first w_mod row: TensorE waited until 11.08 for its third chunk, which x's pieces precede, so that ScalarE's copies of the row start at 14.17 where the forecast had them done at 13.6.
- **The wait for head 3.** Right in place, cause and size: forecast 5 us of ScalarE and 8 of TensorE, measured 4.93 and 7.33, its load issued at 51.99 (forecast 49.4 plus the issue). Removing it two ways gave 4 to 6 us by the ratios. The Trainium skill (PSUM — Partial Sum Buffer, "Engine vs sequencer instructions") calls the queues of ScalarE, VectorE and GpSimd strict FIFO; the trace agrees: two normalizations, two gate copies and exponential 5 stood behind the split until 55.45.
- **The loop.** Right in kind: maximum, exponential, copy, subtraction, one behind the other. It was mis-sized in single steps. Forecast against measured ends of the copies of tiles 0 to 7: 38.5 and 39.6, 43.7 and 45.7, 48.2 and 50.5, 58.5 and 60.7, 62.3 and 64.6, 66.1 and 69.0, 70.6 and 74.7, 73.3 and 79.0. The start gives 1.1 of the 5.7, step 1 gives 0.9 (one of the root's small operations took 1.12 us on DVE, from 40.41, where the others took 0.16 or 0.17), and steps 5, 6 and 7 give 0.6, 1.2 and 1.6. In steps 5 and 6 the prediction counted only DVE's subtractions for the chunks; ScalarE's copies of the same chunks and TensorE's wait of 2.44 us for the chunks' banks lie in the loop too. Step 7 is the clock's.
- **Clock.** Forecast 1 us by the low level behind the long wait. The low level came there, where the loop of step 4 still took 3.9 us for the 3.8 forecast, and again at 72 to 74 us, where seven products took 2.40 us (0.34 each instead of 0.23), which made TensorE and not the loop late in step 7. That cost some 1.6 us: tiles 8 to 10 took 8.6 us, 7.0 in the profiles with the full clock. So the 1 us was near by luck, for it was forecast behind another wait. The Trainium skill's rule (TensorE: Matmul & The Clock Gate, "HAM oscillation — how this bites in real kernels") that a burst behind a wait begins slow agrees with the stretches at 38 and 60 us (0.50 in both). At 72 us the burst had begun at full clock (three products of scores 8 in 0.95 us) and fell in its course, and behind the 2.75 us of the opening the clock stayed at 1.00; these do not agree with it.
- **Sum.** Forecast 0 + 1 at tile 10 (73.3 and 1.6 make 74.9 there, not quite the 75.2), measured 4.2. The terms that were mis-sized are ScalarE's and TensorE's share of steps 5 and 6 (1.8 us), the start (1.1), step 1 (0.9) and step 7's clock (1.6); 1.4 came back, since the projection forecast behind step 7's copy ran mostly ahead of it (copy done at 79.0, scores 10 at 79.5). That is the rival of the longer loop (3146), taken too small.
- **Behind the opening.** Forecast 0 for the background within 4. The stall near 530 us moved instead of going. The further 3.3 us between the profiled spans behind tile 16 (3148.3 - 100.0 against 3140.8 - 95.8) have no place that I can name. In the profile of `slot4` they are gone (3144.8 - 100.8, 3044.0 us), but its ratio hardly moves, so that the slots are their cause isn't shown. The same stretch took 3043.4 us in the profile of `unheld` and 3052.2 in that of `unheld_b`, one kernel run twice, so one execution's chance can hold all of it.
- **Rivals.** The faster one, a kernel without that wait, was priced at 5.6 us (half a us more than the 5 us taken off 75.2); undoing the wait gave 4 to 6, though from 3150 and not from 3143.5. The slower one did not happen in its place: the granted clock from 24 to 36 us was 1.00.
- **What was not weighed** is what the written order itself costs. The prediction took the copy behind the exponential as given. Three changes of place in the queues bring back all of the loss and some 3 us more (ratio 1.0025 to 0.9989).

That the result lies in the range owes something to its width: 3135 to 3152 reaches into both rivals, and the sum itself was some 7 us short.

Still open: what the remaining 5.8 us from P to tile 10 between `spread` and the scheduler's order consist of. A fifth raw buffer, a third way to remove the wait, wasn't tried, and no run takes back the gate's ten products or the two more Wo instances, which the prediction put at nothing.
